# Window attention with a gated feed-forward layer: all engines' orders laid out anew, from a queue model that counts more of PE's instructions

## The chip, the cores and the metric

The kernel runs on one core of one Trainium2 chip. The metric is the device time of one execution in microseconds (us), the median over several runs. Engines are named as in the profile: PE (TensorE matmul; its weight loads stand as PEld), DVE (VectorE), ACT (ScalarE), POOL (GpSimd), SP (the engine that issues all DMAs here).

## The reference

```python
# q, k, v: (8, 8, 576, 64);  window = 64
scores = scale * np.matmul(q, k.transpose(0, 1, 3, 2))
rel = pos[:, None] - pos[None, :]
scores = np.where((rel >= 0) & (rel < window), scores, -1e9)
attn = np.exp(scores - np.max(scores, axis=-1, keepdims=True))
attn = attn / (np.sum(attn, axis=-1, keepdims=True) + 1e-09)
x = attention output, heads joined: (8, 576, 512)
# conv_w: (5, 512); w_val, w_out: (512, 512)
gate_pre = causal convolution of x over the sequence, 5 taps, each channel for itself
gate = 1 / (1 + np.exp(-gate_pre))
out = (gate * (x @ w_val)) @ w_out
```

## The kernel before

The eight batches are worked on in a stream. A unit of attention is `w` (0 to 15): two pairs of heads, half a batch. For each `w` PE makes the scores in two groups `S(w, 0)` (5 tiles of queries) and `S(w, 1)` (4 tiles), line 744. DVE adds the mask and takes the maximum (`M`, line 765), ACT takes the exponentials (`X`, line 777), DVE the reciprocals of the sums (`R`, lines 783 and 785), POOL or ACT scales (`N`, lines 797 and 795), DVE transposes (`T`, line 803), and PE multiplies by the values (`AV`, line 827, four pieces of one `w`). `XH` and `EX` (lines 503 and 506, on ACT or DVE) copy the result out of PSUM, `XL` (line 874, POOL) makes a remainder, so that the later fp32r matmuls lose no precision. The convolution of a pair of heads is one multiplication on ACT (line 939) and four on DVE (`C`, line 941); only the first two pairs of heads do it on PE (`K`, line 906, 10 matmuls of two passes for each half).

Per batch there are eight groups of 12 matmuls `V` (`x @ w_val`, line 979), a sigmoid on ACT (`SIG`, line 1133), eight products `HF` on DVE (line 990), their high and low parts `HH` and `HL` (ACT or DVE, and POOL, line 1008), and four or five groups of 12 matmuls `O` (the product with `w_out`, line 1045), each with a copy `EO` and a store. The `float64` weights come as pairs of integers: eight blocks `w0` to `w7` (and a small `cw`) are each turned into a high and a low part in nine steps `h k b c H p l r s` on DVE, ACT and POOL (`split_f64`, lines 660 to 699). `k` is the clamp of line 665, on DVE or POOL.

PSUM has two buffers for scores, two for `AV` and two for everything else, so `S(w, g)` waits for both `M` of the group before it, and a `V` group waits for the `HF` of the second group before it.

Nothing of the order is written by hand. Every operation is an `Op` with engines it may use, a cost in ns for each, and a priority, which is a formula plus an offset from the table `tw`. `in_order` takes the operation that can start first and so gives each engine its list; the program is emitted in that order. The engines run their lists in order, and SP its DMAs. For PE, `run` keeps an account of the queue of instructions: `words` says how many instructions an operation puts in, and every 256 words a new piece must have come from memory, no sooner than `fetch` ns after the last one. PE also runs matmuls on a tile that nobody reads (`spare`, line 1151) while it has no work at the start.

Of the kernel before, what the change touches and what calls it, by code (L numbers as in the profile page):

```python
# [1200 lines left out]
```

## Time and profile before

| | us |
|---|---|
| median of 3 runs | 350.0 (349.89 to 353.26) |
| the profiled execution | 353.11 |
| its span, first to last instruction | 351.24 |
| outside the span | 1.87 |
| PE busy (matmul) | 325.2 (93% of the span) |
| DVE, ACT, POOL busy | 266.0, 262.4, 155.6 |
| mean granted TensorE clock | 0.961 |

The profile's rows carry times in us. Busy time of PE overlaps from one matmul to the next, so what a matmul costs is read from the chain of waits, where the pieces don't overlap. "issue" is time in which an engine waited for nothing that the profile shows.

### The profile page before, as it was taken

Reading aid. Unit: us, or ns where it says so; the run is one execution under the profiler, and the core shown is the slowest. Engines: PE = TensorE matmul, PEld = TensorE weight load, DVE = VectorE, ACT = ScalarE, POOL = GpSimd, SP = SyncE. Lnnn points to the kernel's source line nnn. Section 1 sums busy time; section 2 is a strip of 40 time slices with the busy share of each in tenths; the row PEclk is TensorE's granted clock in tenths of the full one; section 3 lists DMA queues with packets and bytes.
Section 4 is the critical chain, followed back from the end, with each engine's and each line's share of the span. In section 5 each row is a group of like instructions: output and inputs, shape, how many; then the busy total and the mean of one; then the engine's idle time right before and its main releaser. Section 6 shows DMA issues by size and latency. Waiting matters only on the chain.

```text
span 351.2 us, 15055 instructions
## 1 busy us (share of the span) xinstructions
PE 325.2 (93%) x6154; PEld 270.5 (77%) x6154; DVE 266.0 (76%) x995; ACT 262.4 (75%) x906; POOL 155.6 (44%) x179
## 2 busy tenths in 40 slices
PE   8995986888999999999989998999999999989996
PEld 3443764877788987789869876898889788968985
DVE  6999499978887998799858778698759885863200
ACT  1886688799888998898549888699868967844312
POOL 3244556368715471358134633356446434540510
PEclk9997797896999999999989999999999999999999
DMA  7987661424272527451724128432821240002012
GB/s 256 394 222 232 172 187 39 153 67 137 75 236 73 181 75 217 137 167 44 235 84 142 64 74 255 135 129 55 256 88 33 62 144 34 0 33 91 2 60 90
DMA packets 28228, 45.03 MB, mean 128 GB/s; under 512 B 3968, under 2 KB 15488, under 8 KB 28160
## 3 DMA queue, kind: packets, MB, share of 16 engines
q1 hardware_dynamic: 28160, 44.08, 40.0%
q8 instruction: 48, 0.79, 0.9%
q14 instruction: 20, 0.16, 0.1%
HBM read 34.62 MB, written 9.44 MB: 125 GB/s over the span
## 4 chain that ended last, share of the span: by engine, by line
PE 76%; DVE 6%; DMA 6%; ACT 4%; issue 4%; SPq 3%; ACTq 0%
PE o L1045 30%; PE v L979 27%; PE av L827 9%; PE s L744 7%; DMA st<-in_w_out_dram 3%; PE g L906 3%; DVE gp L941 2%; DMA st<-in_w_val_dram 2%; SPq L611 2%; DVE p L765 2%; ACT p L777 1%; DMA ktb<-in_kT_dram 1%; ACT L777 1%; SPq L592 1%; ACT x L503 1%
## 5 line engine op out<-in xcount | busy, mean ns | idle before, releaser
L777 ACT ACTIVATE p<-p,nm 128x96 f32<-128x96 f32 x288 | 104.1, 367 | 3.0 <-DVE nm L765 2.7
L941 DVE SCALAR_TENSOR_TENSOR gp<-av,cw,gp 128x575 f32<-128x575 f32 (+3 forms) x120 | 92.5, 802 | 3.8 <-ACT x L503 2.2
L979 PE MATMUL v<-xl,wv_hi 128*128 128x288 f32 x256 | 80.0, 312 | 0.8 <-DVE ot L506 0.4
L979 PE MATMUL v<-xh,wv_hi 128*128 128x288 f32 x256 | 77.3, 302 | 0.7 <-issue 0.7
L1008 POOL TENSOR_TENSOR h_lo<-hf,h_hi 128x288 fp32r<-128x288 f32 (+2 forms) x80 | 53.7, 684 | 53.5 <-ACT h_hi L503 47.4
L979 PE MATMUL v<-xh,wv_lo 128*128 128x288 f32 x256 | 76.9, 300 | 0.0
L874 POOL TENSOR_TENSOR xl<-x,xh 128x576 fp32r<-128x576 f32 x32 | 45.3, 1427 | 47.1 <-ACT x L503 15.8
L765 DVE CUSTOM_DVE_ANT_0 p<-s,mask 128x96 f32<-128x96 f32 x288 | 54.4, 251 | 9.3 <-PE s L744 7.9
L1045 PE MATMUL o<-wo_hi,h_lo 128*128 128x512 f32 (+1 forms) x148 | 60.0, 405 | 1.4 <-issue 1.4
L1045 PE MATMUL o<-wo_hi,h_hi 128*128 128x512 f32 (+1 forms) x148 | 58.5, 395 | 2.4 <-issue 2.4
L1045 PE MATMUL o<-wo_lo,h_hi 128*128 128x512 f32 (+1 forms) x148 | 58.4, 395 | 0.7 <-issue 0.7
L797 POOL TENSOR_TENSOR p<-p,rc 128x480 f32<-128x480 f32 (+1 forms) x38 | 34.7, 926 | 50.5 <-DVE rc L785 38.0
L777 ACT ACTIVATION_READ_ACCUMULATOR p<-p,nm 128x1 f32 x288 | 55.2, 192 | 0.0
L979 PEld LDWEIGHTS v<-xl,wv_hi 128*128 128x128 f32 x256 | 50.1, 196 | 4.5 <-DVE hf L990 0.8
L979 PEld LDWEIGHTS v<-xh,wv_lo 128*128 128x128 f32 x256 | 49.8, 195 | 0.8 <-issue 0.8
L979 PEld LDWEIGHTS v<-xh,wv_hi 128*128 128x128 f32 x256 | 50.1, 196 | 0.2
L744 PE MATMUL s<-ktb,qtb 64*32 64x96 f32 x2304 | 38.7, 256 | 10.6 <-DVE nm L765 6.0
L744 PEld LDWEIGHTS s<-ktb,qtb 64*32 64x32 f32 x2304 | 30.2, 108 | 22.8 <-issue 20.3
L827 PEld LDWEIGHTS av<-pts,v 32*64 32x64 f32 x2560 | 35.9, 132 | 11.6 <-issue 9.2
L827 PE MATMUL av<-pts,v 32*64 32x96 f32 (+2 forms) x2560 | 39.9, 246 | 5.0 <-issue 4.3
L803 DVE STREAM_TRANSPOSE pts<-p 128x480 f32<-128x480 f32 (+1 forms) x64 | 38.4, 613 | 7.7 <-POOL p L797 5.4
L990 DVE TENSOR_TENSOR hf<-v,gp 128x288 f32<-128x288 f32 x64 | 28.7, 450 | 15.2 <-PE v L979 15.0
(121 smaller groups left out, 425.2 us busy)
## 6 DMA issues: line engine op xcount, KB each, us to landing
out_dram<-ot SPq DMA_DIRECT2D x35, 256.0 KB, 3.3
qtb<-in_qT_dram SPq DMA_DIRECT2D x30, 288.0 KB, 3.6
ktb<-in_kT_dram SPq DMA_DIRECT2D x30, 288.0 KB, 5.0
v<-in_vw_dram SPq DMA_DIRECT2D x64, 96.0 KB, 3.0
v<-in_vw_dram SPq DMA_DIRECT2D x64, 80.0 KB, 3.4
st<-in_w_val_dram SPq DMA_DIRECT2D x4, 512.0 KB, 6.3
st<-in_w_out_dram SPq DMA_DIRECT2D x2, 1024.0 KB, 6.4
qtb<-in_qT_dram SPq DMA_DIRECT2D x2, 224.0 KB
```

Source lines behind the costliest of these rows:

```text
L744: nc.tensor.matmul(sp_t[m, hh][z * Q:z * Q + Q, t, :], lhsT=held("qt", 2 * w + a)[r, c:c + Q], rhs=held("kt", 2 * w + a)[r, c:c + KW], sta ...
L765: nc.vector.tensor_tensor_reduce(out=pe[:, t, :], in0=sp_t[u][:, t, :], in1=mk[min(n0 + t, 2)], scale=-SCALE, scalar=3.0e38, op0=ALU.add, ...
L777: nc.scalar.activation(out=pe[:, t, :], in_=pe[:, t, :], func=AF.Exp, scale=-1.0, bias=nm[:, t:t + 1], accum_out=su[:, t:t + 1])
L797: MUL[e](out=pe, in0=pe, in1=rc.unsqueeze(2).broadcast_to([P, ng, KW]))
L803: nc.vector.transpose(out=pts_t[w, hh][:, n0 * KW:n1 * KW], in_=p_t.pop(u).rearrange("p t k -> p (t k)"))
L827: nc.tensor.matmul(av_t[2 * w + a][hh * D:(hh + 1) * D, AV0 + lo * Q:AV0 + hi * Q], lhsT=v_t[w][z * Q:z * Q + Q, hh, m % 2, m // 2 - KEYS[ ...
L874: nc.gpsimd.tensor_sub(out=xl[:, hp, :], in0=x_t[i], in1=xh_t[b][:, hp, :].bitcast(F32))
L941: nc.vector.scalar_tensor_tensor(out=acc, in0=x, scalar=col, in1=acc, op0=ALU.mult, op1=ALU.add)
L979: nc.tensor.matmul(vp_t[u][:, 0:NH], lhsT=w[:, c, js], rhs=x[:, c, hs], start=(a + z == 0), stop=(a + z == NM - 1))
L990: nc.vector.tensor_mul(out=hf, in0=vp_t.pop(u)[:, 0:NH], in1=gp_t[b][:, jb, hs])
L1008: SUB[e](out=h_lo[:, jb, dst:dst + hi - lo], in0=hf_t[u][:, lo:hi], in1=h_hi[:, jb, dst:dst + hi - lo].bitcast(F32))
L1045: nc.tensor.matmul(op_t[key][:, 0:cs.stop - cs.start], lhsT=h[:, jb, col:col + P], rhs=w[:, jb, cs], start=(a + z == 0), stop=(a + z == NM ...
```

## The change

The arithmetic and the counts of operations stay: 64 `V`, 37 `O`, 16 `w` of attention, 120 `C` on DVE, 4 `K`. What changes is the planner's model, some rules, and with them every engine's list.

- PE's queue: a scores operation, the first piece of an `AV`, a `K`, a `V` and an `O` count about one word more (for the semaphore instruction); the time from one piece to the next is 5500 ns for the first 40 us and 4100 ns after, where it was 3700; the starting points of the two accounts move (`phases`).
- The clamp costs 250 + 1700 ns on POOL in the plan, where it was 250 + 540. The plan now puts all eight on DVE; before, those of `w4`, `w5` and `w6` were on POOL.
- `x`, the copy of an attention result in SBUF, becomes a tile for two pairs of heads, still in two buffers, freed when both are done. The tile `dg` for the convolution on PE shrinks to the ten matrices used. The large tiles `xl`, `xh` and `gp` are accounted for one by one.
- All offsets `tw` and the numbers `bias`, `wait` and `stay` are new. Code for halves of a batch (`half=()`, `half_attention`, `conv_half`) is there and not used.

```diff
-    fetch=3700,
-    phases=(35, 91),
+    fetch=(5500, 4100, 40000),
+    phases=(55, 71),
-    bias=dict(V=332.09, A=-504.29, G=200.0),
-    wait=13.19,
-    stay=437.83,
+    bias=dict(V=254.51, A=-339.53, G=200.0),
+    wait=0,
+    stay=163.87,
     tw={
-        'LQ0_0': -29.49, 'LQ0_1': -12.62, 'LV0': 43.65,
+        'LQ0_0': -91.82, 'LQ0_1': -5.74, 'LV0': 97.8,
...
-            if at + CFG["fetch"] > x:
-                if at + CFG["fetch"] - x > CFG["rest"]:
-                    cold = at + CFG["fetch"] + CFG["warm"]
-                x = at + CFG["fetch"]
+            there = at + CFG["fetch"][at > CFG["fetch"][2]]
+            if there > x:
+                if there - x > CFG["rest"]:
+                    cold = there + CFG["warm"]
+                x = there
...
-        k = op(name + "k", pick("WK", V=70 + 270 * c, G=250 + 540 * c), clamp, [a], prio=prio, port="VG")
+        k = op(name + "k", pick("WK", V=70 + 270 * c, G=250 + 1700 * c), clamp, [a], prio=prio, port="VG")
...
-        so = prev["S"] = op(f"S{m}", ("P", 165 * ng + 30), e_s, loads + [prev.get("S")],
+        so = prev["S"] = op(f"S{m}", ("P", 165 * ng + 130), e_s, loads + [prev.get("S")],
...
-                            prio=prio, mode="Q", words=32 * ng)
+                            prio=prio, mode="Q", words=32 * ng + 1)
...
-                           free=[], prio=prio, words=2 * len(part))
+                           free=[], prio=prio, words=2 * len(part) + 0.63)
...
-                x_t[i] = sb("x", [P, S], f"x{i}")
-                COPY[e](out=x_t[i], in_=av(i))
+                if i % 2 == 0:
+                    x_t[i // 2] = sb("x", [P, 2, S], f"x{i}")
+                COPY[e](out=x_t[i // 2][:, i % 2, :], in_=av(i))
```

What this moves is seen in the programs' rows. The first place is DVE's list between the last transpose of `w` 1 (`pts1_1`) and the masks of the score group `S(2, 1)` (`p2_1_0`). Before:

```order
L803 STREAM_TRANSPOSE pts1_1_690<-p1_1_1_547 128x384
L660 TENSOR_SCALAR w4m_792<-st2_218 128x512
L765 ISA p2_1_0_809,nm2_1_0_808<-s2_1_0_755,mask_2_85 128x96
L765 ISA nm2_1_0_808 128x1
L765 ISA p2_1_0_809,nm2_1_0_808<-s2_1_0_755,mask_2_85 128x96
L765 ISA nm2_1_0_808 128x1
```

With the change:

```order
L834 STREAM_TRANSPOSE pts1_1_692<-p1_1_1_498 128x384
L707 SCALAR_TENSOR_TENSOR w7l_595<-st3_244,w7m_594 128x512
L692 TENSOR_SCALAR w4a_614<-w4m_615 128x512
L719 TENSOR_TENSOR w7m_594<-w7a_593,wo_hi_119 128x512
L697 SCALAR_TENSOR_TENSOR w4a_614<-st2_124,w4a_614 128x512
L722 TENSOR_TENSOR wo_lo_120<-w7m_594,w7l_595 128x512
L814 TENSOR_SCALAR su2_0_728<-su2_0_728 128x10
L816 RECIPROCAL rc2_0_789<-su2_0_728 128x10
L683 TENSOR_SCALAR w5m_799<-st2_124 128x512
L796 ISA p2_1_0_810,nm2_1_0_809<-s2_1_0_752,mask_2_85 128x96
```

Between the transpose and the masks one step of a weight block (`w4m`) stood; now seven steps of `w7`, `w4` and `w5` and the reciprocals of `S(2, 0)` stand there.

The second place is DVE's list behind the masks of the first half of the score group `S(4, 0)` (`p4_0_0`); those of its second half (`p4_0_1`) free the PSUM that `S(4, 1)` needs. `gp1` are multiplications `C` of the second batch, `hf0` the products `HF` of the first. Before:

```order
L941 SCALAR_TENSOR_TENSOR gp1_1288<-av4_1129,cw_121,gp1_1288 128x575
L941 SCALAR_TENSOR_TENSOR gp1_1288<-av5_1130,cw_121,gp1_1288 128x575
L990 TENSOR_TENSOR hf0_0_3_1338<-v0_0_3_1298,gp0_789 128x288
L941 SCALAR_TENSOR_TENSOR gp1_1288<-av5_1130,cw_121,gp1_1288 128x574
L941 SCALAR_TENSOR_TENSOR gp1_1288<-av4_1129,cw_121,gp1_1288 128x574
L990 TENSOR_TENSOR hf0_1_0_1359<-v0_1_0_1323,gp0_789 128x288
L941 SCALAR_TENSOR_TENSOR gp1_1288<-av5_1130,cw_121,gp1_1288 128x573
L941 SCALAR_TENSOR_TENSOR gp1_1288<-av4_1129,cw_121,gp1_1288 128x573
L765 ISA p4_0_1_1384,nm4_0_1_1383<-s4_0_1_1239,mask_0_83 128x96
```

With the change:

```order
L796 ISA p4_0_0_1286,nm4_0_0_1285<-s4_0_0_1220,mask_2_85 128x96
L796 ISA nm4_0_0_1285 128x1
L1077 SCALAR_TENSOR_TENSOR gp1_1282<-av2_0_1114,cw_121,gp1_1282 128x575
L796 ISA p4_0_1_1313,nm4_0_1_1312<-s4_0_1_1221,mask_0_83 128x96
L796 ISA nm4_0_1_1312 128x1
L796 ISA p4_0_1_1313,nm4_0_1_1312<-s4_0_1_1221,mask_1_84 128x96
L796 ISA nm4_0_1_1312 128x1
L796 ISA p4_0_1_1313,nm4_0_1_1312<-s4_0_1_1221,mask_2_85 128x96
```

Between the two halves there were six `C` and two `HF`; now there is one `C`.

The third place is PE's list at the end of the `AV` of `w` 10 (tiles `av20`, `av21`, with the change `av10_0`, `av10_1`) and the output tile of row 1664 (`o1664`). Before:

```order
L827 MATMUL av21_4013<-pts10_1_3689,v10_1229 64x64
L827 MATMUL av20_4012<-pts10_0_3683,v10_1229 64x32
L827 MATMUL av20_4012<-pts10_1_3689,v10_1229 64x32
L827 MATMUL av21_4013<-pts10_0_3683,v10_1229 64x32
L827 MATMUL av21_4013<-pts10_1_3689,v10_1229 64x32
L1045 MATMUL o1664_0_4109<-wo_hi_119,h_lo_122 128x512
L1045 MATMUL o1664_0_4109<-wo_hi_119,h_hi_123 128x512
```

With the change:

```order
L1184 MATMUL o1664_0_4095<-wo_lo_120,h_hi_123 128x512
L1184 MATMUL o1664_0_4095<-wo_hi_119,h_lo_122 128x512
L1184 MATMUL o1664_0_4095<-wo_hi_119,h_hi_123 128x512
L1184 MATMUL o1664_0_4095<-wo_lo_120,h_hi_123 128x512
L865 MATMUL av10_0_4020<-pts10_0_3648,v10_3839 64x64
L865 MATMUL av10_0_4020<-pts10_1_3667,v10_3839 64x64
L865 MATMUL av10_1_4021<-pts10_0_3648,v10_3839 64x64
```

The 12 matmuls of `o1664` stood behind all four pieces of the `AV`; now they stand ahead of its last piece.

## Rows read from the trace of the kernel before

**Rows 1.** Who PE waited for: us in total, times, longest.

```profile
PE s L744 <- DVE nm L765: 6.0, 3, 3.4
...
PE v L979 <- DVE ot L506: 0.4, 1, 0.4
```

**Rows 2.** The chain that ended last, in order of time: start, us, what. PE's pieces called "issue" behind 91 us.

```profile
91.83 0.77 issue
...
139.87 0.69 issue
...
177.93 1.53 issue
...
217.78 1.61 issue
...
256.35 0.74 issue
...
292.74 0.71 issue
...
308.54 1.40 issue
```

**Rows 3.** Windows from the end of one such piece to the end of a later one: length, then busy us and number of instructions of PE and of PEld, then DVE, ACT, POOL, the granted clock and DMA.

```profile
92.60:140.56 47.96, 47.26 (x1017) 40.17 (x1017) 42.25 (x159) 43.47 (x147) 21.87 (x26) 1.00 0.51 155
...
293.45:309.83 16.38, 15.09 (x255) 14.68 (x254) 10.33 (x20) 12.47 (x39) 9.16 (x10) 1.00 0.01 2
```

**Rows 4.** DMA queues, packets, MB and share: of the whole span, and of the stretch from 177.2 to 178.2 us.

```profile
q8 instruction: 48, 0.79, 0.9%
...
q8 instruction: 1, 0.02, 5.8%
```

**Rows 5.** The chain: stretches of PE's work without a wait, at the full clock.

```profile
153.01 1.13 PE s L744 x69
154.14 6.55 PE v L979 x48
160.69 2.19 PE av L827 x111
...
168.44 5.80 PE o L1045 x24
```

**Rows 6.** Window behind the 1.53 us piece: length, PE busy, granted clock, DMA.

```profile
180.20:183.60 3.40, 3.40 (x10) 0.50 0.40 100
```

**Rows 7.** Timeline of PE up to 82 us: start, us, what; in brackets the idle time before it and what ended it.

```profile
34.82 1.82 PE L744 MATMUL s<-ktb,qtb 64*32 64x96 f32 x72 [2.19 <-DMA ktb<-in_kT_dram]
36.57 4.46 PE L906 MATMUL g<-x,dg 128*128 128x288 f32 x10
...
43.15 2.68 PE L906 MATMUL g<-x,dg 128*128 128x288 f32 x10
...
80.46 1.09 PE L744 MATMUL s<-ktb,qtb 64*32 64x96 f32 x62 [2.32 <-DVE nm L765]
```

**Rows 8.** Timeline of SP: start, us of issuing, what. Eight loads of values for `w` 1, and the first load of the last pair for `S(2, 0)`.

```profile
24.84 5.61 SPq L611 DMA_DIRECT2D v<-in_vw_dram  x8
30.54 0.53 SPq L592 DMA_DIRECT2D qtb<-in_qT_dram  x1
```

**Rows 9.** Timeline of DVE: the masks of `S(2, 1)`, and the first two `HF`.

```profile
43.27 0.26 DVE L765 CUSTOM_DVE_ANT_0 p<-s,mask 128x96 f32<-128x96 f32 x1 [3.92 <-PE s L744]
...
69.44 0.81 DVE L990 TENSOR_TENSOR hf<-v,gp 128x288 f32<-128x288 f32 x2
```

**Rows 10.** Groups of DVE's instructions by form: busy us, mean ns of one, idle time before.

```profile
L990 DVE TENSOR_TENSOR hf<-v,gp 128x288 f32<-128x288 f32 x64 | 28.7, 450 | 15.2 <-PE v L979 15.0
...
L941 DVE SCALAR_TENSOR_TENSOR gp<-av,cw,gp 128x574 f32<-128x574 f32 x30 | 23.9, 803 | 0.1
...
L803 DVE STREAM_TRANSPOSE pts<-p 128x480 f32<-128x480 f32 x32 | 20.8, 662 | 1.4 <-POOL p L797 1.1 <-ACT p L795 0.2
...
L506 DVE CAST xh<-av 128x576 fp32r<-128x576 f32 x11 | 8.2, 746 | 7.1 <-ACT x L503 5.9 <-PE av L827 1.1
...
L506 DVE CAST h_hi<-hf 128x288 fp32r<-128x288 f32 x5 | 1.6, 324 | 0.0
...
L684 DVE SCALAR_TENSOR_TENSOR w4l<-st,w4m 128x512 f32<-128x512 uint32 x1 | 0.7, 684 | 0.0
...
L665 DVE TENSOR_SCALAR w1m<-w1m 128x512 f32<-128x512 f32 x1 | 0.4, 422 | 0.0
```

**Rows 11.** The chain: mask steps of DVE, each from its start to the start of the next.

```profile
53.03 0.17 DVE p L765
53.21 0.17 DVE p L765
```

**Rows 12.** Timeline of POOL: a clamp.

```profile
59.66 2.08 POOL L665 TENSOR_SCALAR w5m<-w5m 128x512 f32<-128x512 f32 x1 [1.21 <-DVE w5m L660]
```

**Rows 13.** The chain up to the first output tile.

```profile
88.71 1.57 PE av L827 x86
90.28 1.12 PE s L744 x69
91.41 0.43 PE o L1045
```

**Rows 14.** Window from the first output tile to the last "issue" piece: busy us and instructions of PE, PEld, DVE, ACT, POOL.

```profile
91.34:308.54 217.20, 210.61 (x4329) 182.46 (x4324) 175.77 (x660) 179.29 (x617) 100.05 (x115) 0.99 0.39 121
```

More of the change, by code (lines that the diff above doesn't have):

```diff
@@ L490, in tile_window_attention_gated_ffn, with place, pairs_of @@
     PS, SB = CFG["ps"], CFG["sb"]
+    HALF = CFG["half"]
+    def place(w, z):
+        b, y = divmod(w, 2)
+        if b in HALF:
+            return b * NHP + z, y
+        return 2 * w + z // 2, z % 2
+    def pairs_of(w):
+        return sorted({place(w, z)[0] for z in range(P // Q)})
     const = ctx.enter_context(tc.tile_pool(name="const", bufs=1))
@@ L540, in tile_window_attention_gated_ffn @@
             nc.vector.memset(mk[n][z * Q:z * Q + Q, 0:W - n * Q], NEG / SCALE)
+    mh = [const.tile([P, KW], F32, name=f"mask_h{n}") for n in range(2 if HALF else 0)]
+    for n, t in enumerate(mh):
+        nc.vector.tensor_copy(out=t, in_=mk[2])
+        nc.vector.memset(t[:, 0:W - n * Q], NEG / SCALE)
     wv_hi = const.tile([P, NC_, DM], F32R, name="wv_hi")
@@ L583, in load_qk @@
         b, hp = divmod(i, NHP)
-        cuts = (0, CFG["cut"], S) if i < 2 and CFG["cut"] else (0, S)
+        cuts = (0, NH, S) if b in HALF else (0, CFG["cut"], S) if i < 2 and CFG["cut"] else (0, S)
         loads = []
@@ L601, in load_v @@
     def load_v(w):
[L602 removed]
+        b = w // 2
         def emit(_):
@@ L733, in scores @@
         last = n1 == NQ
+        half = w // 2 in HALF
+        gone = pairs_of(w) if last and not (half and w % 2 == 0) else []
         def e_s(_):
@@ L804, in scores, with count @@
             tr_of.setdefault(w, []).append(
-                op(f"T{u}", ("V", 80 + 104 * ng), e_t, [no] + tr_of.get(w, [])[hh:hh + 1] * (g > 0), take=[("pts", (w, hh))] if g == 0 else [],
+                op(f"T{u}", ("V", 80 + 104 * ng), e_t,
+                   [no] + (tr_of[w][hh:hh + 1] if g else tr_of.get(w - 1, [])[hh:hh + 1]), take=[("pts", (w, hh))] if g == 0 else [],
                    free=[("p", u)], prio=prio))
     def products(w):
-        steps = list(range(NQ + 2))
+        half, y = w // 2 in HALF, w % 2
+        steps = list(range(NQ if half and y == 0 else NQ + 2))
         cuts = sorted({min(c, len(steps)) for c in CFG["avs"]})
         ao = prev.get("AV")
+        def count(z, t):
+            th = place(w, z)[1]
+            m = th * (NQ - 2) + t
+            return th, m, max(m, th * NQ), min(m + 3, th * NQ + NQ), m < (th + 1) * NQ
         for k0, k1 in zip(cuts, cuts[1:]):
@@ new lines, in products @@
+            top = max(x[3] - x[0] * NQ for r in live for x in r if x[4])
+            trs = [o for g in range(len(PARTS) - 1) if PARTS[g] < top for o in tr_of[w][2 * g:2 * g + 2]]
+            words = sum(8 * x[4] for r in live for x in r)
+            cost = sum(CFG["nav"] if all(x[4] for x in r) else 100 for r in live)
+            ao = prev["AV"] = op(f"AV{w}_{k0}", ("P", cost), e_av, trs + [lv_of[w], ao],
+                                 take=[("ps_av", (w, a)) for a in range(2)] if k0 == 0 else (),
@@ new lines, in half_attention, with src, e_ex, e_fr @@
+    def half_attention(w, cwo):
+        b, y = divmod(w, 2)
+        ao = products(w)
+        s = (2 * w + 1) * NB * PB
+        t0 = y * NH
+        gates = []
+        for a in range(2):
+            i = b * NHP + 2 * a
+            pr = slice(2 * a, 2 * a + 2)
+            def src():
+                return av_t[w, a].rearrange("p (h n) -> p h n", n=512)[:, :, 0:NH]
+            def e_ex(e, a=a, i=i):
+                if y == 0:
+                    x_t[i // 2] = sb("x", [P, 2, S], f"x{i}")
+                COPY[e](out=x_t[i // 2][:, :, t0:t0 + NH],
+                        in_=av_t[w, a].rearrange("p (h n) -> p h n", n=512)[:, :, 0:NH])
+            ex = op(f"EX{i}_{y}", pick("EX", A=535, V=665), e_ex, [ao], take=[("x", i // 2)] if y == 0 else [], prio=s)
+            def e_fr(_, a=a):
+                del av_t[w, a]
+            op(f"FR{i}_{y}", ("N", 0), e_fr, [ex], free=[("ps_av", (w, a))], prio=s)
+            def e_xh(e, i=i, pr=pr):
+                xh = batch_tile(xh_t, "xh", b, F32R)
+                COPY[e](out=xh[:, pr, t0:t0 + NH], in_=x_t[i // 2][:, :, t0:t0 + NH])
+            big = [(n, b) for n in ("xl", "xh", "gp")] if y == 0 and a == 0 else []
+            xh_o = op(f"XH{i}_{y}", pick("XH", A=535, V=375), e_xh, [ex, prev.get("XH")], take=big, prio=s, port="VG")
+            prev["XH"] = xh_o
+            def e_xl(e, i=i, pr=pr):
+                xl = batch_tile(xl_t, "xl", b, F32R)
+                SUB[e](out=xl[:, pr, t0:t0 + NH], in0=x_t[i // 2][:, :, t0:t0 + NH],
+                       in1=xh_t[b][:, pr, t0:t0 + NH].bitcast(F32))
+            xl_o = op(f"XL{i}_{y}", pick("XL", V=665, G=180 + 2.07 * S), e_xl, [xh_o], prio=s, port="VG")
+            xh_ops.setdefault((b, y), []).extend([xh_o, xl_o])
+            for j in range(i, i + 2):
+                gates.append(conv_half(j, y, ex, xh_o, cwo, s))
+            if y:
+                freed(i // 2, [xl_o] + gates[-2:], s)
+        return gates
@@ new lines, in conv_half, with e_cv, e_cc, emit @@
+    def conv_half(i, y, ex, xh_o, cwo, s):
+        b, hp = divmod(i, NHP)
+        cp = s + CFG["cp0"][i % len(CFG["cp0"])]
+        t0 = y * NH
+        x = lambda lo, hi: x_t[i // 2][:, i % 2, lo:hi]
+        if CFG["conv"][i:i + 1] == "K":
+            def e_cv(_):
+                g = gc_t[i, y] = ps("f", [P, 512], f"g{i}_{y}")
+                for kk in range(TAPS - 1, -1, -1):
+                    back = TAPS - 1 - kk
+                    lo = back if y == 0 else 0
+                    nc.tensor.matmul(g[:, lo:NH], lhsT=dg[:, (KP.index(hp) * TAPS + kk) * P:(KP.index(hp) * TAPS + kk + 1) * P],
+                                     rhs=x(t0 + lo - back, t0 + NH - back), start=back == 0, stop=kk == 0)
+            cv = op(f"K{i}_{y}", ("P", 500 * TAPS), e_cv, [ex, dgo[hp], xh_o], take=[("ps_f", (i, y))],
+                    words=4 * TAPS + 1, prio=cp)
+            def e_cc(e):
+                COPY[e](out=batch_tile(gp_t, "gp", b, F32)[:, hp, t0:t0 + NH], in_=gc_t.pop((i, y))[:, 0:NH])
+            o = op(f"CC{i}_{y}", pick("CC", A=300, V=369), e_cc, [cv], free=[("ps_f", (i, y))],
+                   prio=cp)
+        else:
+            o = None
+            for kk in range(TAPS - 1, -1, -1):
+                def emit(_, kk=kk):
+                    back = TAPS - 1 - kk
+                    lo = back if y == 0 else 0
+                    acc = batch_tile(gp_t, "gp", b, F32)[:, hp, t0 + lo:t0 + NH]
+                    src = x(t0 + lo - back, t0 + NH - back)
+                    col = cw[:, hp * TAPS + kk:hp * TAPS + kk + 1]
+                    if back == 0:
+                        nc.scalar.activation(out=acc, in_=src, func=AF.Copy, scale=col)
+                    else:
+                        nc.vector.scalar_tensor_tensor(out=acc, in0=src, scalar=col, in1=acc, op0=ALU.mult, op1=ALU.add)
+                o = op(f"C{i}_{y}_{kk}", ("A", 395) if kk == TAPS - 1 else ("V", 400), emit,
+                       [o, cwo] + ([ex, xh_o] if kk == TAPS - 1 else []),
+                       prio=cp, port="G" if kk == TAPS - 1 else "VG")
+        return o
@@ L924, in e_cc @@
                         COPY[e](out=acc, in_=g)
-                    if half:
-                        del x_t[i]
                 last.append(op(f"CC{i}_{half}", pick("CC", A=335, V=369) if not end else ("V", 440 + 70 * (1 - half)),
-                               e_cc, [cv], free=[("ps_f", (i, half))] + ([("x", i)] if half and end else []), prio=cp))
+                               e_cc, [cv], free=[("ps_f", (i, half))], prio=cp))
+            released(i, [xl_o] + last, s)
             return [xh_o, xl_o], last
@@ L943, in emit @@
                 if kk == 0:
-                    del (x_t if own else av_t)[i]
+                    if not own:
+                        del av_t[i // 2, i % 2]
             return emit
@@ L949, in attention @@
                    [o, cwo, xl_o if kk == 0 else None] + (x_ready if kk == TAPS - 1 else []),
-                   free=[("x" if own else "ps_av", i)] if kk == 0 else [], prio=cp,
+                   free=[("ps_av", i)] if kk == 0 and not own else [], prio=cp,
                    port="VG" if own else "G")
+        if own or CFG["xl"][i] != "V":
+            released(i, [xl_o] + ([o] if own else []), s)
         return [xh_o, xl_o], [o]
@@ L1018, in ffn @@
         last_v = ops_by_prefix(f"V{b}_", f"HF{b}_")
-        op(f"CB{b}", ("N", 0), lambda _: None, last_v, free=[("big", (b, n)) for n in range(3)], prio=prio)
+        op(f"CB{b}", ("N", 0), lambda _: None, last_v, free=[(n, b) for n in ("xl", "xh", "gp")], prio=prio)
         if odd:
@@ new lines, in gate, with e_sig @@
+    def gate(b, ops_, prio, t0=0, t1=S):
+        def e_sig(_):
+            g = gp_t[b][:, :, t0:t1]
+            nc.scalar.activation(out=g, in_=g, func=AF.Sigmoid)
+        return op(f"SIG{b}_{t0}", ("A", 95 + 500 * NHP * (t1 - t0) / S + 2580), e_sig, ops_, prio=prio + CFG["sig_prio"])
+    for b in range(B):
+        x_ops, sig = {}, {}
+        if b in HALF:
+            for y in range(2):
+                w = 2 * b + y
+                for g in range(len(PARTS) - 1):
+                    scores(w, g)
+                gates = half_attention(w, cwo)
+                x_ops[y] = xh_ops[b, y]
+                sig[y] = [gate(b, gates, (2 * w + 2) * NB * PB, y * NH, y * NH + NH)] * NHP
+        else:
+            xs, cs = [], []
+            for hp in range(NHP):
+                i = b * NHP + hp
+                if i % 2 == 0:
+                    for g in range(len(PARTS) - 1):
+                        scores(i // 2, g)
+                x, c = attention(i, cwo)
+                xs.extend(x)
+                cs.extend(c)
+            x_ops = {0: xs, 1: xs}
+            sig[0] = sig[1] = [gate(b, cs, (b + 1) * NHP * NB * PB)] * NHP
+        ffn(b, x_ops, sig, w_ops, (b + 1) * NHP * NB * PB + CFG["ffn_prio"])
```

149 lines of the change are left out of this document (71 added, 78 removed), and 489 rows, old and new, of the table tw.

## The prediction

> **What bounds the kernel now.** I read the waits of PE, then the chain in order of time, then windows and timelines. PE is busy 93% of the span. Behind 91 us the chain runs on PE almost alone, and DVE makes it wait 0.4 us there [rows 1]; what interrupts PE are seven pieces called "issue", 0.77, 0.69, 1.53, 1.61, 0.74, 0.71 and 1.40 us, together 7.45 us [rows 2]. Ahead of 91 us PE waits for DVE's masks (6.0 us in three waits) and for a load [rows 1, 7].
>
> What ends an "issue" piece is not named, but the rows tell. Between the ends of two of them stand 1017 + 1017, or 255 + 254, matmuls and weight loads [rows 3]. With the semaphore instructions, which these counts leave out, these are 8 and 2 times 256. The instruction queue brought 48 packets with 0.79 MB, 16.4 KB each [rows 4], for 2 x 6154 matmuls and weight loads: 256 a packet. In the microsecond in which the 1.53 us piece begins there is one such packet [rows 4]. So PE stops where a packet of its own program is late. How soon one is used up depends on what is in it: an `AV` unit has 320 instructions for 2.19 us, so 256 of them are 1.75 us of work; 12 matmuls of `O` are 24 instructions and 2.9 us, 12 of `V` 1.64 us [rows 5].
>
> **The seven stops.** I counted both PE lists in pieces of 256 instructions, from the place of the stops on, and priced each piece [rows 5] (for a group of scores 1.13 us; the smaller by its tiles). Before, the pieces behind the eleventh with the least work hold 2.0, 3.1, 1.75, 1.7, 2.7, 1.75, 2.0 and 1.75 us, and all but the one of 1.7 end in one of the seven stops. Work and stop together are 2.5 to 4.3 us. So a piece with 4.3 us of work should never stop. With the change the smallest piece behind the eleventh holds 4.4 us: `AV` is cut by an `O` or a `V`, as with `o1664`, or stands at another place in the count. Term: **-7.45 us**; bounds -7.45 and, if a third of the pieces still ends late, -5.
>
> Behind the 1.53 us stop the granted clock is 0.50 for 3.4 us, the lower level of 1.2 GHz, with PE busy throughout [rows 6]. Half of it is lost work, 1.7 us. Without the stop I expect no drop there: **-1.7 us** (bounds -1.7 and 0).
>
> **The start.** The first output tile begins at 91.4 us [rows 13]. I work out when it begins with the change; it is `O128`, behind `S(5, 0)`, which needs all masks of `S(4, 1)`.
>
> `S(2, 0)` waits for its last load and starts at 34.8 [rows 7]. Before, SP issues 8 loads of values, a pair of `q` and `k`, 8 loads of values and the last pair [rows 8]; with the change 16 loads of values (for `w` 0 and 4) and then both pairs. What stands ahead of the last pair is the same, so 34.8 stays, and 36.6 for the end. Then PE has two groups of the convolution, 4.4 us at the low clock and 2.7 at the full one [rows 7], and `S(2, 1)`, 1.0: done at 44.7. Before it was 43.2, but DVE stood idle for 3.92 us there [rows 9]. Now it has the seven weight steps of the first place in those microseconds, which came later before. They are hidden behind PE; if `S(2, 1)` came early, they would cost their 3 to 4 us.
>
> From 44.7 DVE's list up to the first `HF` has 26 mask steps of 0.18 [rows 11], 8 `C` of 0.80, 6 transposes of 0.66 at most, 10 short steps (eight of weights, two `R`) of 0.42, 5 long ones of 0.68 and 2 copies of 0.75 [rows 10]: 4.6 + 6.4 + 3.8 + 4.2 + 3.4 + 1.5 = 23.9 us, so 68.6, where it was 69.4 [rows 9]. That contains the clamps of `w5` and `w6`, now two short steps on DVE instead of 2 us each on POOL [rows 12]; of weight work nothing is left on DVE behind it, while before a long step and a difference (0.68 each) followed.
>
> From the first `HF` to the last mask of `S(4, 1)`: 18 mask steps, 8 `C`, 7 `HF` of 0.45, a transpose, two `R` and a copy of 0.32: 3.2 + 6.4 + 3.2 + 0.7 + 0.8 + 0.3 = 14.6 us, so 83.2; `S(5, 0)` ends 1.1 later, 84.3. PE is there in time. The second place is the reason: `S(4, 1)` waited for the second half of the masks until 80.46, six `C` and two `HF` behind the first half [rows 7], and all `V` groups of the batch behind it. Now one `C` stands between, and I get 72.4 for it (68.6, two `HF`, a copy, 5 masks, a `C`, 5 masks). The remaining `V` groups, 1.64 each, follow the `HF` one by one. The first two pieces of 256 around `AV` of `w` 2 hold 1.8 and 2.3 us and would stop PE, but PE waits there anyhow: for masks until about 61 and for the `C` that free the `AV` tiles until 63.
>
> So the first output begins 7.1 us sooner, with three pieces of an `AV` unit (1.57 us, rows of before [rows 13]) still to do: **-5.5 us** net. Bounds: if each DVE step is priced from start to start (some 0.07 us less each, 55 steps) it is -9; if PE is late by other waits, 0.
>
> **New waits.** Behind the first output PE has the same work in 9 us less. DVE is busy 176 of 217 us there and ACT 179 [rows 14], which rises to 85%. The nearest row for what this costs is the 0.4 us of before, the farthest the 6.0 us of the start [rows 1]. I take +1.5, nearer to the first, as each stop taken away was 0.7 to 1.6 us and gave DVE that much to catch up.
>
> **The sum.** 351.2 - 7.45 - 1.7 - 5.5 + 1.5 = 338.0 us of span, and 1.9 around it: 339.9. The profiled execution (353.1) lies 3.1 above the median, 350.0; no row tells where these 3.1 us are. If in the stops, they go with them and 339.9 stands; if elsewhere, it is 336.8. I take the middle, **338.3 us**.
>
> **Rivals.** (a) The stops go and the start gains nothing: DVE is what paces it, its steps are the same, and three more clamps are on it. Against this is the hole of 3.92 us. 338.3 + 5.5 = 343.8.
>
> (b) The stops don't come from the lists of instructions but stay, or come back elsewhere: 338.3 + 9.15 = 347.5. Against this are the counts of 256. The Trainium skill's page "Runtime: NRT & Kernel Launch", section "Instruction fetch mechanics", speaks for it: the sequencer fetches the next block of 256 instructions while it works on the current one, and crossing a block costs little that shows. By that rule the new order could gain only at the start. The trace agrees with the 256 and not with the rest, at ten places with short instructions.
>
> (c) Slower: DVE becomes the bound in every batch, since each `V` group waits for an `HF` two groups back and DVE's `C` of the next batch stand between the `HF`. For it speaks the 81% that DVE is busy [rows 14]; against it the 0.4 us of waits. It decides from 1.9 us of new waits a batch: eight times that is 15.2, and 338.3 + 15.2 = 353.5.
>
> (d) All of it moves little: the start loses what the stops give, 350.
>
> **How the numbers follow.** The forecast, with its own range of 333 to 342, has 0.66, (a) 0.14, (b) 0.08, (c) 0.06, (d) 0.06. The range from 333 to 346 takes in the forecast and (a); the lower end is the sum with -9 for the start, no new waits and 336.8 as its base. About 1% is what a measurement of this kernel can tell from no change: 346.5 and 353.5. Forecast and (a) are faster, with a little of (b): 0.82; (b) and (d) the same: 0.12; (c) slower: 0.06.
>
> **What would show it.** Right: behind the first output no "issue" piece on PE over 0.5 us, the granted clock at 1.00 from there to the end, the first output at 82 to 86 us, the masks of `S(2, 1)` at 45 us with under 2 us of waiting before them, `S(4, 1)` at 71 to 75. Wrong: stops that stand at new places, at pieces of over 4 us of work; `V` or `S` waiting for DVE by more than 4 us in all behind the first output; a first output at 90 or later, or `S(2, 0)` starting much behind 35 because a load of values came ahead of it.

## The result, and the profile after

| | before | with the change |
|---|---|---|
| median, us | 349.94 (348.76 to 353.26, 4 runs) | 339.65 (339.09 to 340.64, 4 runs) |
| ratio, 95% interval | | 0.9694 (0.9625 to 0.9764) |
| span of the profiled execution | 351.24 | 338.10 |
| PE busy | 325.2 | 315.7 |
| mean granted TensorE clock | 0.961 | 0.973 |

The change makes the kernel 3.1% faster. 338.3 us, faster, was forecast, and it is faster, by 1.35 us less than that. The terms added up to 338.0 us of span, and 338.10 was measured; that this is so near is partly luck, as will be seen. Medians here and below are over all runs; ratios leave out runs that lie over 1.5% above the fastest of the same kernel (two of four of `shift64`, two of ten of `shift32`, one of four of `loads`).

Who PE waited for in the kernel with the change, from the view of waits (us in total, times, longest), in answer to [rows 1]:

```profile
PE s L775 <- DVE rc L816: 4.2, 1, 4.2
PE s L775 <- DVE nm L796: 3.5, 5, 1.2
PE s L775 <- DMA ktb<-in_kT_dram: 2.5, 1, 2.5
PE av L865 <- issue: 2.1, 2, 1.4
...
PE v L1118 <- ACT ot L516: 0.7, 1, 0.7
PE v L1118 <- issue: 0.7, 1, 0.7
```

All three waits called "issue" lie ahead of 72 us. In the chain of this kernel, in order of time, the two longest pieces called "issue" behind 72 us are these; the seven of [rows 2] have no successor.

```profile
80.46 0.21 issue
...
281.06 0.22 issue
```

PE's timeline of the same kernel at the places of [rows 7] and the first output: the first two rows are `S(2, 0)`, which goes on at 37.16, then come `S(4, 1)` and `O128`.

```profile
34.10 0.54 PE L775 MATMUL s<-ktb,qtb 64*32 64x96 f32 x8 [4.24 <-DVE rc L816]
37.16 1.83 PE L775 MATMUL s<-ktb,qtb 64*32 64x96 f32 x72 [2.51 <-DMA ktb<-in_kT_dram]
...
74.06 1.00 PE L775 MATMUL s<-ktb,qtb 64*32 64x96 f32 x64
...
84.68 0.50 PE L1184 MATMUL o<-wo_hi,h_lo 128*128 128x512 f32 x1
```

DVE's timeline at the places of [rows 9]: the masks of `S(2, 0)`, those of `S(2, 1)`, and the first two `HF`.

```profile
39.02 0.26 DVE L796 CUSTOM_DVE_ANT_0 p<-s,mask 128x96 f32<-128x96 f32 x1 [3.74 <-PE s L775]
...
45.58 0.26 DVE L796 CUSTOM_DVE_ANT_0 p<-s,mask 128x96 f32<-128x96 f32 x1 [0.39 <-PE s L775]
...
69.21 0.80 DVE L1129 TENSOR_TENSOR hf<-v,gp 128x288 f32<-128x288 f32 x2
```

The first output begins at 84.68 where 84.3 was forecast, but on another way. The wait of 3.92 us that DVE had ahead of the masks of `S(2, 1)` is 0.39; in its place it waits 3.74 ahead of those of `S(2, 0)`, since that group goes on at 37.16 and not at 34.82. So the first `HF` comes at 69.21, no sooner than the 69.44 of before. What is won at the start is won behind the first `HF`: `S(4, 1)` starts at 74.06 instead of 80.46.

The windows from the first output to the end of the span (length, then busy us and instructions of PE, PEld, DVE, ACT, POOL, the granted clock, DMA). Before:

```profile
91.34:351.24 259.90, 248.90 (x4545) 216.18 (x4540) 187.63 (x679) 193.91 (x644) 109.92 (x129) 0.99 0.35 110
```

With the change:

```profile
84.68:338.10 253.42, 248.82 (x4654) 216.72 (x4652) 187.30 (x683) 197.29 (x658) 111.12 (x129) 1.00 0.36 113
```

PE's idle time in these windows falls from 11.00 to 4.60 us; the granted clock behind the first output is 1.00 with the change.

### The profile page after: what moved, and what is told of

Its sections match the earlier page's. It is cut to its first block, busy times and chain, and to the rows that moved or that the text cites. A ratio compares the mean times of both kernels' runs of the same rounds, so it can differ in the third digit from the quotient of the medians.

```text
span 338.1 us, 15037 instructions
## 1 busy us (share of the span) xinstructions
PE 315.7 (93%) x6148; PEld 265.6 (79%) x6148; DVE 262.3 (78%) x1000; ACT 261.9 (77%) x904; POOL 148.6 (44%) x175
## 4 chain that ended last, share of the span: by engine, by line
PE 74%; DMA 8%; ACT 7%; DVE 6%; SPq 3%; issue 1%; ACTq 0%; DVEq 0%
PE o L1184 28%; PE v L1118 26%; PE av L865 10%; PE s L775 7%; DMA ktb<-in_kT_dram 4%; DMA st<-in_w_out_dram 3%; ACT p L808 3%; PE g L1043 2%; SPq L628 2%; DVE gp L1077 2%; DVE p L796 1%; DVE pts L834 1%; ACT gp L1075 1%; ACT L808 1%; SPq L609 1%
## 5 line engine op out<-in xcount | busy, mean ns | idle before, releaser
L1118 PE MATMUL v<-xl,wv_hi 128*128 128x288 f32 x256 | 78.7, 308 | 3.7 <-POOL xl L1012 2.0
L1118 PE MATMUL v<-xh,wv_hi 128*128 128x288 f32 x256 | 76.4, 298 | 0.7 <-issue 0.7
L1118 PE MATMUL v<-xh,wv_lo 128*128 128x288 f32 x256 | 76.0, 297 | 0.0
L1012 POOL TENSOR_TENSOR xl<-x,xh 128x576 fp32r<-128x576 f32 x32 | 46.0, 1445 | 37.7 <-ACT x L516 14.6
L1184 PE MATMUL o<-wo_lo,h_hi 128*128 128x512 f32 (+1 forms) x148 | 57.7, 390 | 0.0
L1184 PE MATMUL o<-wo_hi,h_hi 128*128 128x512 f32 (+1 forms) x148 | 57.6, 389 | 0.0
L1118 PEld LDWEIGHTS v<-xl,wv_hi 128*128 128x128 f32 x256 | 49.0, 191 | 7.1 <-POOL xl L1012 2.2
L1118 PEld LDWEIGHTS v<-xh,wv_hi 128*128 128x128 f32 x256 | 49.0, 191 | 1.1 <-issue 0.9
L1118 PEld LDWEIGHTS v<-xh,wv_lo 128*128 128x128 f32 x256 | 48.8, 191 | 0.0
```

Source lines behind the costliest of these rows:

```text
L1012: nc.gpsimd.tensor_sub(out=xl[:, hp, :], in0=x_t[i // 2][:, i % 2, :], in1=xh_t[b][:, hp, :].bitcast(F32))
L1118: nc.tensor.matmul(vp_t[u][:, 0:NH], lhsT=w[:, c, js], rhs=x[:, c, hs], start=(a + z == 0), stop=(a + z == NM - 1))
L1184: nc.tensor.matmul(op_t[key][:, 0:cs.stop - cs.start], lhsT=h[:, jb, col:col + P], rhs=w[:, jb, cs], start=(a + z == 0), stop=(a + z == NM ...
```

## The experiments

The first two ask what the stops hang on. `shift64` leaves every list of the change as it is and only adds 64 instructions to PE ahead of `S(2, 0)`:

```diff
+    more = {"S(2, 0)": 16}
     for o in order:
+        for _ in range(more.get(o.name, 0)):
+            nc.tensor.matmul(spare[0:32, 0, 0:8], lhsT=ident[0:64, 0:32], rhs=ident[0:64, 0:8], start=True, stop=True)
```

> The changed kernel with 16 narrow spare matmuls (64 instructions of PE, some 2 us in a wait of 6.7 us) ahead of S(2, 0), nothing else. Every piece of 256 instructions behind them starts 64 instructions earlier in the program. Theory (stops come from pieces of 256 instructions with little work): ten pieces behind the first output now hold under 3.3 us of work, eight of them 1.75 to 2.5; at 0.93 us each (7.45 us for eight in the kernel before) 7.4 us of stops, and up to 3 us at the lower clock: 347.5 us (345 to 350), the first output at 84 to 86 us as before. Rival (the order of the work gives the time, the count doesn't matter): 339.7 (339 to 341).

Measured: 359.55 us (353.82 to 362.73). The two runs that count, 353.82 and 358.73, are too few for a ratio; both are above the 351.22 us of the kernel before beside them and far above the change. Its window behind the first output, and the longest "issue" pieces of its chain there:

```profile
88.55:356.90 268.35, 252.95 (x4657) 219.38 (x4652) 189.53 (x682) 196.99 (x652) 111.49 (x129) 0.99 0.34 107
```

```profile
107.20 1.54 issue
...
125.55 1.86 issue
...
141.16 1.73 issue
...
253.65 3.04 issue
...
292.45 1.62 issue
```

The stops are back, and they cost more than expected: the stretch is 14.9 us longer than with the change alone, 10.8 of it idle time of PE (15.40 against 4.60) and 4.1 more time shown as busy. The first output is 3.9 us later too, which the 64 instructions may have caused themselves, or which may be scatter of the start (more of that below).

`shift192` goes the other way. It keeps the old order of all work and replaces the six wide spare matmuls ahead of `S(1, 0)` by 54 narrow ones, 192 instructions more:

```diff
+    more = {"S(1, 0)": 54}
...
-        for _ in range(getattr(o, "spares", 0)):
+        for _ in range(0 if o.name in more else getattr(o, "spares", 0)):
```

> The kernel before with the 6 wide spare matmuls (24 instructions, 5.4 us) ahead of S(1, 0) replaced by 54 narrow ones (216 instructions), so the pieces of 256 start 192 instructions earlier in the program; the order of all work is that of before. Theory: no piece behind the first output holds under 3.4 us of work, so the seven stops (7.45 us) and the drop of the clock (1.7 us) are gone: 340.8 us (339 to 343), most of the gain of the whole change. Rival (the new order gives the gain): 350 (348.5 to 352).

Measured: 340.46 us (338.89 to 343.24), ratio 0.9735 (0.9649 to 0.9822). Its window behind the first output, and all that PE waited for behind 92 us:

```profile
89.26:338.10 248.84, 245.45 (x4544) 214.62 (x4540) 187.46 (x679) 193.70 (x644) 109.97 (x129) 1.00 0.36 115
```

```profile
PE v L979 <- DVE ot L506: 0.4, 1, 0.4
```

With the same matmuls behind the first output, in the same order as before, the stretch is 11.06 us shorter: idle time from 11.00 to 3.39, busy time from 248.90 to 245.45. So this shift alone, with no operation moved, gives about what the whole change gives.

`shift32` asks the same of the change with half the shift, and without touching its start (the first output is at 85.29): 3 of 7 wide spare matmuls ahead of `S(0, 1)` become 11 narrow ones.

```diff
+    more = {"S(0, 1)": 11}
...
-        for _ in range(getattr(o, "spares", 0)):
+        for _ in range(getattr(o, "spares", 0) - 3 * (o.name in more)):
```

> The changed kernel with 3 of the 7 wide spare matmuls (12 instructions) ahead of S(0, 1) replaced by 11 narrow ones (44), so that the pieces of 256 behind start 32 instructions earlier in the program; at that place PE waits for loads, so the start should not move. Theory: four pieces behind the first output hold 1.75 to 2.4 us and one 2.7; with 64 instructions eight pieces of 1.75 to 2.5 cost 15 us behind the first output (12.1 of stops, the rest in slower matmuls), so about half: 346.5 us (344 to 350). Rival (what shift64 showed came from its delayed start): 339.7 (339 to 341).

Measured: 351.3 us (347.95 to 354.95), ratio 0.9999 (0.9953 to 1.0045): 32 instructions take the whole gain away, more than was expected. The profiled execution is the shortest of its ten. In it PE is idle 8.86 us in the stretch behind the first output, 4.3 more than with the change, and busy 3.2 us longer:

```profile
85.29:346.20 260.91, 252.05 (x4657) 218.87 (x4652) 189.15 (x682) 196.49 (x652) 111.45 (x129) 0.99 0.35 110
```

`o1664` undoes one stop of before, by the third place of the change:

```diff
-    order = in_order(ops, room)
+    order = follow(in_order(ops, room), room, [(["O1664_0_0"], "AV10_9")])
```

Here and below, `follow` moves the operations named ahead of the one named last, on their engine alone; all other lists stay as they were.

> The kernel before with one group moved on PE alone: the 12 matmuls of the output tile of row 1664 from behind the last piece of the AV of w 10 to ahead of it, as the change has it. The count of instructions ahead of every other operation stays. Theory (a stop belongs to a piece of 256 instructions with little work): that piece's work goes from 2.7 to over 3.4 us, so the stop of 1.61 us at 217.8 goes and the other six stay: 1 to 2 us shorter, 348.6. Rival: it stays or goes elsewhere, 350.

Measured: 350.2 us, ratio 0.9985 (0.9959 to 1.001). In its chain the stop between 177.93 and 256.35 of [rows 2] is gone and its neighbours are there, with no piece over 0.5 us between them:

```profile
175.65 1.69 issue
...
251.90 0.68 issue
```

The stop went as expected. The time did not follow: 0.5 us, with an interval that ends just short of the 1.6 that the stop had taken in one execution.

Two kernels measure the packets by themselves, with 2048 instructions behind the last output. `tiny` has 512 matmuls, all on one place of the array:

```diff
         o.emit(o.engine)
+    tiny = ps("f", [P, 4, P], "tiny")
+    for _ in range(512):
+        nc.tensor.matmul(tiny[0:32, 0, 0:8], lhsT=ident[0:64, 0:32], rhs=ident[0:64, 0:8], start=True, stop=True)
```

> The changed kernel with 512 tiny matmuls (64 x 32 by 64 x 8, fp32, 4 instructions each, 2048 in all, eight pieces of 256) behind the last output; their result is not read. Theory (a packet of 256 instructions takes some 3 to 3.7 us to come, measured as the shortest time between two places of the same count): they run at about 3.3 us a piece with a stop every 256 instructions, 8 x 3.3 = 26 us at the end, span 364. Rival (bringing instructions is hidden): they run at the rate of the scores, 160 instructions in 1.13 us, 14.5 us in all, without stops, span 352.

Its span is 389.6, 51.5 more than with the change, without stops. The trace counts each of these matmuls twice (1024 in all). On one place 104 of them take 3.30 us at the full clock, which makes 4.1 us for 256 instructions (128 matmuls), and 191 take 10 us at the granted clock of 0.50, which makes 6.7. By themselves they are slower than the 3.0 to 3.7 us that a packet was expected to take, so the kernel tells nothing of the packets. `tiny2` goes round eight places:

```diff
+    tiny = [ps("f", [P, 4, P], f"tiny{n}") for n in range(2)]
+    for n in range(512):
+        r = slice(64 * (n % 2), 64 * (n % 2) + 64)
+        c = 32 * (n // 2 % 4)
+        nc.tensor.matmul(tiny[n % 2][c:c + 32, 0, 0:96], lhsT=ident[r, c:c + 32], rhs=ident[r, 0:96], start=True, stop=True)
```

> The changed kernel with 512 short matmuls behind the last output (64 x 32 by 64 x 96, fp32, over eight places of the array in turn, as the scores have them; 2048 instructions, eight pieces of 256); their result is not read. The earlier try used one place of the array and was too slow by itself (5.8 to 6.4 us a piece) to show a stop. Theory: at 1.8 us of work a piece the packets pace them, with a stop every 256 instructions, 3.0 to 3.7 us a piece, 24 to 30 us in all. Rival (bringing instructions is hidden): 1.8 us a piece, 14.3 us in all, no stops.

The span is 364.8, 26.7 more than with the change. PE's timeline there; a row is a run of matmuls, each with a weight load, and in brackets the idle time ahead of it:

```profile
340.64 1.72 PE L1305 MATMUL tiny<-ident 64*32 64x96 f32 x128 [1.86 <-issue]
344.37 1.72 PE L1305 MATMUL tiny<-ident 64*32 64x96 f32 x128 [2.01 <-issue]
348.37 2.02 PE L1305 MATMUL tiny<-ident 64*32 64x96 f32 x128 [2.29 <-issue]
352.10 2.81 PE L1305 MATMUL tiny<-ident 64*32 64x96 f32 x128 [1.71 <-issue]
355.55 2.11 PE L1305 MATMUL tiny<-ident 64*32 64x96 f32 x128 [0.64 <-issue]
359.01 1.72 PE L1305 MATMUL tiny<-ident 64*32 64x96 f32 x128 [1.35 <-issue]
362.48 1.22 PE L1305 MATMUL tiny<-ident 64*32 64x96 f32 x83 [1.75 <-issue]
```

There is a stop every 128 matmuls, each with its weight load, which is exactly 256 instructions, and from start to start 3.73, 4.00, 3.73, 3.45, 3.46 and 3.47 us pass, whatever the work in between (1.72 to 2.81; the longest lies in a window, 350 to 355 us, with a granted clock of 0.50). That is the price of a packet by itself, 3.64 us in the mean.

Three kernels undo parts of the start, each on the change. `hole` puts seven DVE operations back behind the masks of `S(2, 1)`: `R(2, 0)` and the weight steps of the first place, of which there are six (they were counted as seven):

```diff
-    order = in_order(ops, room)
+    order = follow(in_order(ops, room), room, [(["w7l", "w4b", "w7r", "w4c", "w7s", "R(2, 0)", "w5h"], "w5k")])
```

> The changed kernel with seven DVE steps (w7l w4b w7r w4c w7s R(2, 0) w5h) moved from ahead of the masks of S(2, 1) to behind them, as they roughly stood before; no other engine's list differs. Theory (those steps fill time in which DVE waits for PE): DVE idles 3 to 4 us ahead of these masks and everything up to the first output comes that much later: 343 us (341.5 to 344.5), first output at 87.5 to 89. Rival (the start is bound elsewhere, by loads or PE, and these steps have slack): 339.7 (338.5 to 341).

Measured: 344.95 us (342.96 to 346.29), ratio 0.985 (0.9767 to 0.9934), just above the expected range. DVE's timeline, the masks of `S(2, 0)`, of `S(2, 1)`, and the first `HF`:

```profile
38.47 0.26 DVE L839 CUSTOM_DVE_ANT_0 p<-s,mask 128x96 f32<-128x96 f32 x1 [3.20 <-PE s L818]
...
45.03 0.26 DVE L839 CUSTOM_DVE_ANT_0 p<-s,mask 128x96 f32<-128x96 f32 x1 [3.74 <-PE s L818]
...
74.06 0.81 DVE L1172 TENSOR_TENSOR hf<-v,gp 128x288 f32<-128x288 f32 x2
```

DVE now waits at both places: the steps do fill the wait. The first `HF` is 4.85 us later than in the profile of the change. Part of this is scatter: in `tiny2`, `tiny` and `dve`, which have the change's lists up to there, it comes at 70.56, 71.22 and 71.62, so that 2.4 to 3.5 us are left.

`mask` puts the second half of the masks of `S(4, 0)` back:

```diff
-    order = in_order(ops, room)
+    order = follow(in_order(ops, room), room, [(["M((4, 0), 1)"], "HF0_0_1")])
```

> The changed kernel with the masks of the second half of S(4, 0) moved back behind six C and two HF on DVE, as they stood before; no other engine's list differs. Theory (these masks free the PSUM of S(4, 1) and all V groups behind it): S(4, 1) starts 5 to 6 us later, the first output 3 to 5 us later, and the end keeps some 0.7 of that, as it did of the delay in hole: 342.5 us (341 to 344). Rival (DVE has the same work anyhow, so only its order changes): 339.7 (338.5 to 340.7).

Measured: 345.09 us (342.31 to 346.64), ratio 0.9811 (0.9731 to 0.989), which overlaps a little with that of the change; this too is above the expected range. In PE's timeline `S(4, 1)` waits again:

```profile
76.75 1.04 PE L818 MATMUL s<-ktb,qtb 64*32 64x96 f32 x62 [3.64 <-DVE nm L839]
```

The wait of 3.64 us is what the masks hold up. That the group goes on 2.7 us later than with the change shows less: with nothing moved it begins at 76.78 in `tiny` and at 77.44 in `tiny2`.

`clamps` puts three clamps back on POOL:

```diff
+    for o in order:
+        if o.name in ("w4k", "w5k", "w6k"):
+            o.engine = "G"
```

> The changed kernel with the clamps of w4, w5 and w6 on POOL, as before, instead of DVE; all else in the new order. Theory (the sum counted them as three short DVE steps of 0.42 us in place of 2.1 us each on POOL): DVE's next step of each block waits for POOL, 1 to 3 us up to the first output: 341.5 us (340.5 to 343). Rival (the clamps are hidden on either engine): 339.7 (338.5 to 340.4).

Measured: 340.8 us (337.77 to 341.99), ratio 0.9723 (0.9637 to 0.981). It can't be told from the change; whether the clamps cost 1 us or nothing stays open.

`dve` tests rival (c), DVE as the next bound:

```diff
+        if o.name[:2] == "HF" and o.name[2] != "0" and o.name[3:] in ("_0_0", "_0_2", "_1_1", "_1_3"):
+            nc.vector.scalar_tensor_tensor(out=pad, in0=pad, scalar=cw[:, 0:1], in1=pad, op0=ALU.mult, op1=ALU.add)
         o.emit(o.engine)
```

> The changed kernel with 28 extra steps on DVE, a multiply-add of 128 x 287 on a tile that nobody reads, ahead of four of the eight HF of each batch from the second on; 0.45 us each by the HF, 12.6 us in all, 1.8 a batch. Theory (DVE is not the bound behind the first output, 187 of 253 us busy): most of it is hidden, 341.5 us (340 to 344). Rival (rival (c) of the prediction: DVE is the bound in every batch): nearly all of it shows, 350 (347 to 353).

Measured: 345.9 us (345.5 to 347.21), between the two: about half of the 12.6 us shows. DVE is not the bound, but it is near.

`loads` tries to better the start, at the load that `S(2, 0)` waits for. It issues the last two pairs of `q` and `k` ahead of the eight loads of values for `w` 4:

```diff
-    order = in_order(ops, room)
+    order = follow(in_order(ops, room), room, [(["LQ4_0", "LQ5_0"], "LV4")])
```

> The changed kernel with the last two pairs of q and k that S(2, 0) needs issued ahead of the eight loads of values of w 4, instead of behind them; no other engine's list differs. Theory (the start is paced by this load and then by DVE's list behind S(2, 0)): S(2, 0) starts 2 to 4 us earlier than 37.2, the first output 1 to 3 us earlier than 84.7, of which the end keeps 0.5 to 2: 338.3 us (337.3 to 339.3). Rival (DVE's list alone paces the start, and it is full): 339.7 (339 to 340.5).

Measured: 336.16 us (335.13 to 340.76), ratio 0.958 (0.9551 to 0.9609), the fastest of all by the median; the interval lies below that of the change. `S(2, 0)` runs whole at 31.72, and the first output is at 81.69:

```profile
31.72 1.26 PE L818 MATMUL s<-ktb,qtb 64*32 64x96 f32 x80
...
81.69 0.50 PE L1227 MATMUL o<-wo_hi,h_lo 128*128 128x512 f32 x1
```

`shift192loads` asks whether the old order takes the same help: `shift192` with one load moved.

```diff
-    order = in_order(ops, room)
+    order = follow(in_order(ops, room), room, [(["LQ5_0"], "LV1")])
```

> shift192 (the old order of all work, with the pieces of 256 shifted) and one more move: the last pair of q and k for S(2, 0) is issued ahead of the eight loads of values of w 1 instead of behind them. Theory (the new order is worth nothing beyond the place of the pieces; the start is paced by this load and by DVE's list): as in loads, 1.5 to 3.5 us less than shift192's 340.5, so 338 us (336.5 to 339.5), as good as the whole change. Rival (the new order of DVE at the start is needed for it, the old list has no work to fill the time that an earlier S(2, 0) gives): 340.5 (339.5 to 341.5).

Measured: 340.67 us (338.61 to 342.0), ratio 0.9711 (0.9665 to 0.9756), nothing gained over `shift192`. The theory put on record there is wrong: the first output is at 88.95, as without the load. The rival can't be seen in its own terms, since `S(2, 0)` came no earlier. Its larger part starts at 37.44, behind a stop of 1.58 us, and at 36.58 in `shift192`. But DVE comes to the masks of `S(2, 0)` at 39.94 (39.78 in `shift192`), from other work and without a wait, so an earlier `S(2, 0)` would have found it busy. As far as this goes, the early load pays only with the new order: 336.16 against 340.67 us.

## Why the prediction was right

**The stops.** This step was right and its size too. Packets of 256 instructions pace PE where a piece holds little work: the same order gains 11.06 us behind the first output by a shift of 192 instructions, and the new order loses 14.9 there by one of 64. Of the term of -7.45, 7.6 is measured as PE's idle time (11.00 to 3.39 us, `shift192`). Rival (b) fell with it. The Trainium skill ("Runtime: NRT & Kernel Launch", section "Instruction fetch mechanics") says that crossing a block costs little that shows. `tiny2` does not agree: it measures 3.64 us a block, and 1.7 us of work hides only half of that.

**The clock.** -1.7 was put down for one stretch at 0.50, but in `shift192` PE's busy time falls by 3.45 us (248.90 to 245.45) for the same matmuls. The stretch of [rows 6] is half of it. The rest is not the clock: in windows of 5 us the granted clock of before is 1.00 everywhere behind the first output but in the window from 180 us, shown here. So the clock was sized rightly, and a term of 1.75 us was put at nothing.

```profile
180.00:185.00 5.00, 5.00 (x78) 3.78 (x79) 3.13 (x5) 1.35 (x3) 1.42 (x1) 0.66 0.39 103
```

Part of the term is lost overlap, as at the 1.61 us stop:

```profile
217.16 0.40 PE L1045 MATMUL o<-wo_lo,h_hi 128*128 128x512 f32 x1
217.39 0.39 PE L1045 MATMUL o<-wo_hi,h_lo 128*128 128x512 f32 x1
219.40 0.50 PE L1045 MATMUL o<-wo_hi,h_hi 128*128 128x512 f32 x1 [1.61 <-issue]
```

The first of these matmuls is shown as 0.40 us long, but the second starts 0.23 later; the second has none behind it, so its whole 0.39 counts, 0.16 more. For seven stops this makes an estimated 1.1 us, if the others are like it; what the rest is stays open.

**The start.** -5.5 was forecast; 91.34 to 84.68, less the 1.57 of `AV` work still to do, is -5.1. That this was met is luck (see the offset, below), and one step failed: "What stands ahead of the last pair is the same, so 34.8 stays". The bytes are the same, but both pairs now stand one right behind the other at the end. The chain has the last load, from its issue to its landing, at

```profile
31.56 5.46 DMA ktb<-in_kT_dram
```

where before it had landed when `S(2, 0)` went on at 34.82 [rows 7]. This load takes 4.43 to 5.58 us in the nine profiles with the new order of loads, and 3.57 to 4.67 in three with the old one. But not all of the delay comes from the order: in `shift192` and `o1664`, with the old one, `S(2, 0)` goes on at 36.58 and 36.59, and DVE's wait ahead of the masks of `S(2, 1)` is 0.98 and 2.55 there and not 3.92. So the weight steps filled one wait of DVE and another opened 6 us earlier; `hole` shows that without them both would be there, `loads` that with the load in time neither need be, for 3.5 us. The second place, the masks of `S(4, 0)`, worked as told: `S(4, 1)` came at 74.06 for the 72.4 forecast, and waited 3.64 us for these masks when `mask` undid it.

**New waits.** +1.5 was chosen. Against `shift192`, which has neither stops nor the new order, PE is idle 1.21 us longer with the change (4.60 against 3.39) and busy 3.37 longer, of which 1.57 is the `AV` work: +3.0. Part of it is the wait of 0.7 for a copy of ACT; the rest is spread, and its causes stay open.

**The sum.** -7.6, -3.45, -5.1 and +3.0 make -13.15; the span fell by 13.14. This closes because the four are cut out of the same spans, and says nothing for the terms. The extra busy time, 1.75, was put at nothing and the new waits 1.5 too small, and these cancel. The lower end of the range has a slip: with -9 for the start, no new waits and 336.8 as the base it is 331.8 and not 333.

**The offset of 3.1 us.** It was split down the middle between the stops and the rest. Where the first output begins in each profile with one of the two orders up to there tells more:

- The order of before: 91.34, and 89.26, 89.23 and 88.95 in `shift192`, `o1664` and `shift192loads`.
- The order of the change: 84.68, and 85.29, 86.72, 87.08 and 87.08 in `shift32`, `tiny`, `tiny2` and `dve`. The programs of `tiny` and `tiny2` are the change's up to their last matmuls.

The rows of `shift192`, `o1664`, `tiny` and `tiny2` are, in this order:

```profile
89.26 0.50 PE L1045 MATMUL o<-wo_hi,h_lo 128*128 128x512 f32 x1
...
89.23 0.51 PE L1088 MATMUL o<-wo_hi,h_lo 128*128 128x512 f32 x1
...
86.72 0.50 PE L1184 MATMUL o<-wo_hi,h_lo 128*128 128x512 f32 x1
...
87.08 0.50 PE L1184 MATMUL o<-wo_hi,h_lo 128*128 128x512 f32 x1
```

So the profile of before has the latest start of four, and that of the change the earliest of five. Some 2.1 of the 3.1 us lay in the start of that one execution of before. Set against 89.2, the median of the four, the change's own profile gains 4.6 us at the start, 3.0 net of the `AV` work; the median of the five, 86.7, gains 2.5, or 1.0 net. Neither is 5.1, and which start the timed runs of the change had is not known. The new waits, +3.0, take either back. That is in keeping with the change (339.65) and `shift192` (340.46) ending together: rival (a), the stops go and the start gains nothing, describes the outcome as well as the forecast does. `hole` and `mask`, which lose some 5 us, show that the new order needs its two places at the start, not that it starts so much better than the old one. Rival (a) erred in its price: less the 1.75 of busy time and the 1.5 of new waits, which `shift192` does not have, its 343.8 are 340.55.

## What to carry to other kernels

Count a long list of short matmuls in pieces of 256 instructions from the place of a stop, and price each piece; one with less work than a packet takes to come (3.45 to 4.00 us here) can stop PE, and a few instructions more at the start may be worth as much as a new order of everything. Before a gain is put down to a new order, run the old order with its pieces shifted: the difference between those two is what the order is worth. When a wait is filled, look at what now ends one step earlier, since here the late load behind it was worth another 3.5 us. Take more than one profile for a start: here the first output moved by 2.4 us between programs that are the same up to there.
